# Idle TensorE products at the start of an attention-and-MLP kernel: nineteen in place of twenty-four, and sixteen of them ahead of the first mean product

## The chip, the core and the metric

The kernel runs on one core of one Trainium2 chip. The metric is the device time of one execution in microseconds (us), as the median of several runs; lower is better. Beside the timed runs there is one profiled execution, from which all the views below come. Its span is the time from its first to its last recorded instruction.

## The reference

The kernel computes one mixer block on x with 2048 tokens of 512 features, in float32. A sliding local attention with 32 heads of 16 features looks at 8 earlier positions in steps of 2; an MLP with 1376 hidden features gates it.

```python
xn = layernorm(x)
qkv = xn @ wqkv                                  # 512 -> 3 * 512
logits = q . k[pos - 2*w] * 16 ** -0.5           # w = 0..7, masked where pos - 2*w < 0
s = (softmax(logits) . v[pos - 2*w]) @ wo
h = gelu(layernorm(xn) @ w1 + b1)                # 512 -> 1376
g = silu(h @ w2 + b2)                            # 1376 -> 512
out = x + s * g
```

## The kernel before, in words

**Tiling.** The 2048 tokens are split by parity c (0 or 1) and then into 8 tiles of 128 tokens each. Attention runs in eight units (c, hb), where hb is a block of 8 heads; the MLP runs over four chunks of 512 tokens and eleven blocks of hidden features. Nearly every product on TensorE (PE) is done three times, in float16: each float32 operand is split into a high and a low half, and high·high, high·low and low·high are summed in PSUM. The lines that carry this work are L864 (qkv), L1143 (first MLP product), L1186 (second MLP product) and L1056 and L1088 (the product with wo).

**The start.** Before the float16 halves exist, two tiles of parity 0 (tiles 6 and 7) take another way. They are loaded already transposed (L1258, tensor `in_A_xt_dram`, into `U`), and each is centred: a product with a constant 128x128 matrix of 1/512 (`mean1`, in the tile `first`) gives the mean over the features, and VectorE (DVE) subtracts it in L693. For tile 6 DVE sums the four feature blocks first (L685) and PE multiplies once (L691, the first mean product); for tile 7 PE does four products (L682). The centred tile is multiplied in float32 with the raw weights of hb 0 (L700, four products a tile). The other tiles are loaded by L1233 into `prod` and go through statistics on DVE (L659, L660, L714, L716), a power on GpSimd (POOL, L718), a normalisation on one of three engines (L744 on ScalarE, written ACT here; L748 on POOL; L751 on DVE), a transpose on PE (L766), and the split into halves (L770 or L772 for the high half, L773 for the low half). Only then can L864 use them. The weights of hb 0 get a common scale on the way: ACT sums squares (L597), PE adds these up over the partitions (L513), DVE makes the scale (L524 to L542), ACT and DVE or POOL make the halves (L619; L626 or L553 and L554). Results of L864 leave PSUM by L882 (ACT) or L878 (DVE).

**The idle products.** Line 1305 makes products whose result nobody reads: the stationary operand is the constant tile `fours` (bfloat16, 128x128), the moving operand is `mean1` seen as 256 columns of bfloat16, and the result goes to the PSUM bank z0. They need nothing but the two constants that DVE sets at the start (L439, L440), and, where z0 was used by something else, that its reader is done. Their number is the constant `WAKE`:

```python
for n in range(WAKE):                                          # L1303
    b = R_z[0].new()
    pl.add("pe", 0.2, lambda b=b: nc.tensor.matmul(b.t[:, 0:2 * P], fours, mean1.bitcast(BF16), start=True,
                                                   stop=True), [], [b], prio=1e9)
```

**What sets the order.** All operations are first added to a plan (`Plan.add`), in which each has its number, engine, reads and writes. `Plan.issue` then walks through the tuple `ORDER`, which names every operation once by its number, picks a buffer of each ring for it and issues it on its engine:

```python
order, fixed = [], [self.ops[n] for n in reversed(ORDER)]      # L296
```

So each engine executes its share of `ORDER` in that sequence. An instruction that waits for a semaphore holds up everything behind it on its engine. The loads all go through the queue of SyncE (SP), in the sequence of the tuple `LOADS`, and SP uses eight semaphores in turn, so that the ninth load is issued when the first has landed, and so on.

Of the kernel before, what the change touches and what calls it, by code (L numbers as in the profile page):

```python
# [70 lines left out]
BEFORE_W1 = (0, 1, 4, 5)  # L71

ORDER = (
# [62 lines left out]
)  # L136


class Buf:


    def __init__(self, ring):
        self.ring, self.slot, self.left, self.end = ring, None, 0, 0.0
# [224 lines left out]
PU1 = 0.969  # L368
PWARM = 0.9
PEV = 0.2698  # L370

PTOT = 0.5899

WAKE = 24
PS1 = 1.1561

QHI = 4

PQLO = 0.5225

# [1146 lines left out]
```

## Time and profile before

| what | us |
|---|---|
| median of 3 timed runs | 413.33 (413.10 to 413.67) |
| the profiled execution's own time | 412.45 |
| its span, first to last instruction | 410.6 |
| PE busy in it | 403.6 |
| DVE busy | 381.7 |
| ACT busy | 225.3 |
| POOL busy | 132.8 |

A row of the timeline reads: start and duration in us from the span's start, engine, line, operation, what it writes `<-` what it reads, size, how many in a row, and in brackets the engine's idle time before it with what ended it. Where a row merges several instructions, the duration is that of the whole row. Matmuls are pipelined: each is recorded for longer than the distance to the next, so the rate is read from the distance between starts, not from the duration of one. LDWEIGHTS rows (PEld) are the loading of a stationary operand, beside the matmuls.

### The profile page before, as it was taken

The page shows a single profiled execution, that of the slowest core. Times are in us where ns is not written, and L with a number is a line of the kernel's source. Part 1 is how long each engine was busy: PE and PEld are TensorE (multiplying, and loading weights), DVE is VectorE, ACT ScalarE, POOL GpSimd, SP SyncE. Part 2 cuts the span into 40 slices and gives each one's busy share as a digit, 9 for nine tenths or more (in the row PEclk, how much of TensorE's full clock was granted, in tenths as well). Part 3 has the DMA queues.
Part 4 walks back from the last instruction along what each step waited for, and adds up shares of the span by engine and source line. Part 5 has one row for each costly group of instructions (what it writes and reads, how often), then busy time and mean ns, then how long its engine had stood idle before and what let it go on. Part 6 is the DMA issues. An engine that isn't in the chain of part 4 may idle for free.

```text
span 410.6 us, 5500 instructions
## 1 busy us (share of the span) xinstructions
PE 403.6 (98%) x2035; PEld 199.3 (49%) x2035; DVE 381.7 (93%) x386; ACT 225.3 (55%) x372; POOL 132.8 (32%) x141
## 2 busy tenths in 40 slices
PE   7999999999999999999999999999999999999996
PEld 4665544444444455445544554444445544444443
DVE  4999999999999999999889999899999989989985
ACT  4899987983989736633564164114523177236310
POOL 3833000053552434243423344233322505250012
PEclk9999999999999999999999999999999999999999
DMA  8947437240018372911251008610244462004874
GB/s 300 388 105 233 165 110 199 89 180 26 1 30 197 77 130 79 165 32 27 51 145 23 0 2 215 208 51 25 104 120 122 107 137 59 0 1 117 271 209 180
DMA packets 52627, 48.04 MB, mean 117 GB/s; under 512 B 37066, under 2 KB 37510, under 8 KB 52088
## 3 DMA queue, kind: packets, MB, share of 16 engines
q1 hardware_dynamic: 52600, 47.69, 41.8%
q8 instruction: 16, 0.26, 0.3%
q14 instruction: 11, 0.09, 0.1%
HBM read 24.40 MB, written 7.34 MB: 77 GB/s over the span
## 4 chain that ended last, share of the span: by engine, by line
PE 97%; DVE 1%; DMA 1%; ACT 0%; issue 0%; ACTq 0%; DVEq 0%
PE ps L864 30%; PE ps L1143 25%; PE z L1186 25%; PE ps L1056 5%; PE z L1088 2%; PE ps L1088 2%; PE z L1174 2%; PE pl L864 1%; PE pl L700 1%; DMA U<-in_A_xt_dram 1%; PE pl L1088 1%; PE z L700 1%; PE z L1177 1%; PE z L766 1%; PE z L1305 0%; DVE U L1120 0%
## 5 line engine op out<-in xcount | busy, mean ns | idle before, releaser
L864 PE MATMUL ps<-wq,yT 128*128 128x384 f16 (+1 forms) x708 | 129.3, 337 | 0.1
L1186 PE MATMUL z<-w,h 128*128 128x512 f16 x480 | 111.4, 379 | 0.0
L1143 PE MATMUL ps<-yT,w 128*128 128x512 f16 x480 | 109.1, 379 | 0.0
L864 PEld LDWEIGHTS <-yT 128*128 128x128 f16 x744 | 72.3, 98 | 58.5 <-issue 1.1
L930 DVE TENSOR_TENSOR prod<-U 128x2048 f32<-128x2048 f32 x32 | 73.8, 2312 | 4.1 <-ACT U L882 3.0
L1143 PEld LDWEIGHTS <-w 128*128 128x128 f16 x480 | 46.7, 98 | 55.6 <-issue 0.5
L933 DVE TENSOR_REDUCE L<-prod 128x128 f32<-128x2048 f32 x32 | 73.0, 2282 | 0.5
L1186 PEld LDWEIGHTS <-h 128*128 128x128 f16 x480 | 46.5, 98 | 54.6 <-issue 0.7
L999 POOL TENSOR_TENSOR prod<-prod,prod 128x1024 f32<-128x1024 f32 x14 | 41.3, 2970 | 81.4 <-DVE prod L988 81.4
L882 ACT ACTIVATE U<-ps,cs 128x384 f32<-128x384 f32 x54 | 30.2, 577 | 62.9 <-PE ps L864 62.7
L988 DVE TENSOR_TENSOR prod<-pl,U 128x2048 f32<-128x2048 f32 x28 | 63.5, 2283 | 0.3
L1156 ACT ACTIVATE ps<-ps,b1T,hsc 128x512 f32<-128x512 f32 x40 | 29.9, 748 | 37.2 <-PE ps L1143 37.0
L1159 ACT ACTIVATE h<-ps,hsc 128x512 f16<-128x512 f32 x40 | 27.4, 685 | 20.5 <-PE z L1186 19.5
L1009 POOL COPY gate<-prod 1x1 f32<-1x1 f32 x21 | 4.6, 221 | 102.2 <-DVE prod L930 102.2
L1010 POOL TENSOR_TENSOR prod<-prod 128x1024 f32<-128x1024 f32 x14 | 32.8, 2346 | 0.0
L1161 DVE SCALAR_TENSOR_TENSOR h<-ps,hsc,h 128x512 f16<-128x512 f32 x40 | 29.5, 744 | 3.3 <-ACT h L1159 3.3
L1056 PE MATMUL ps<-wo,oT 128*128 128x512 f16 x96 | 21.5, 379 | 0.0
L983 DVE TENSOR_TENSOR prod<-prod,prod 128x2048 f32<-128x2048 f32 x9 | 20.6, 2288 | 0.2
L971 ACT ACTIVATE o<-prod,osc 128x1024 f16<-128x1024 f32 (+1 forms) x9 | 9.5, 1052 | 18.1 <-DVE prod L983 9.9
L1010 POOL TENSOR_TENSOR prod<-prod,prod 128x1024 f32<-128x1024 f32 x7 | 16.4, 2347 | 0.0
L1088 PEld LDWEIGHTS <-oT 128*128 128x128 f16 x108 | 10.5, 98 | 10.4 <-issue 0.2
L1056 PEld LDWEIGHTS <-oT 128*128 128x128 f16 x96 | 9.4, 98 | 11.1
(201 smaller groups left out, 397.2 us busy)
## 6 DMA issues: line engine op xcount, KB each, us to landing
f<-in_A_x_dram SPq DMA_DIRECT2D x31, 256.0 KB, 3.1
U<-U SPq DMA_DIRECT2D x16, 392.0 KB, 6.2
gd<-f SPq DMA_DIRECT2D x12, 256.0 KB, 4.3
prod<-in_A_x_dram SPq DMA_DIRECT2D x8, 256.0 KB, 6.2
oT<-in_B_w_dram SPq DMA_DIRECT2D x2, 1024.0 KB
yT<-in_B_w_dram SPq DMA_DIRECT2D x2, 1024.0 KB
f<-gd SPq DMA_DIRECT2D x8, 256.0 KB, 5.0
out_dram<-f SPq DMA_DIRECT2D x8, 256.0 KB
```

Of the source, the lines that this page charges most:

```text
L864: nc.tensor.matmul(b.t[:, 0:wide], y[:, s, k, o:o + P], wq[hb][:, t, k], start=(n == 0), stop=(n == 11))
L882: act(384, lambda i=i, b=b: nc.scalar.activation(U3[:, i:i + 31:15, :], b.t[:, 0:384].rearrange("p (t e) -> p t e", t=3), AF.Identity, sca ...
L930: dve(2048, lambda p2=p2, g=g: nc.vector.tensor_tensor(p2(), q, slots(Ut, KH, 2 * g), op=ALU.mult), qk + [("kh", ub, 0), ("kh", ub, 1), (" ...
L933: dve(2048, lambda pr=pr, g=g: nc.vector.tensor_reduce(L3()[:, 2 * g:2 * g + 2], pr.t.rearrange("p (r f d) -> p r f d", r=2, d=DH), AX.X, ...
L988: dve(2048, lambda: nc.vector.tensor_tensor(pr.t.rearrange("p (r f d) -> p r f d", r=2, d=DH), A3()[:, 2 * g:2 * g + 2].rearrange("p r (f ...
L999: pool(2.4, lambda n=n: nc.gpsimd.tensor_tensor(acc.t[:, n:n + 1024], acc.t[:, n:n + 1024], p1.t[:, n:n + 1024], op=ALU.add), [acc, p1], [ ...
L1010: nc.gpsimd.tensor_tensor(x.t[:, 0:1024], x.t[:, 0:1024], y(), op=ALU.add)
L1056: nc.tensor.matmul(b.t, oT[:, hb, i // 4, s, i % 4], wo[:, t, hb], start=(hb == 0 and n == 0), stop=(hb == last and n == 2))
L1088: nc.tensor.matmul(b.t[:, cols], oT[:, hb, i // 4, s, i % 4], wo[:, t, hb, cols], start=(start and hb == 0 and n == 0), stop=(stop and hb ...
L1143: nc.tensor.matmul(b.t[0:M], w1[:, s, f * 512 + k * M:f * 512 + (k + 1) * M], yT[ch][:, t, k], start=(n == 0), stop=(n == 11))
L1156: act(512, lambda: nc.scalar.activation(b.t[0:M], b.t[0:M], AF.Gelu_apprx_tanh, bias=b1T[0:M, f:f + 1], scale=hsc[0:M, 1:2]), [b, ("b1T",) ...
L1186: nc.tensor.matmul(z.t, hl[s][:, t * P:(t + 1) * P], w2[:, w, f], start=(f == 0 and n == 0), stop=False)
```

## The change

`WAKE` goes from 24 to 19, and the idle products stand at other places of `ORDER`. Since five operations fewer are added to the plan, every operation behind them has a number that is lower by five, and so the whole tuple is written anew. The sequence of all other operations is the same: DVE, ACT, POOL and SP execute the same instructions in the same order, and PE the same apart from L1305.

```diff
 ORDER = (
-    0, 1, 240, 19, 2, 3, 4, 5, 6, 7, 8, 9, 10, 11, 133, 129, 113, 120, 112, 115, 130, 20, 21, 32, 33, 168, 114,
+    0, 1, 235, 19, 2, 3, 4, 5, 6, 7, 8, 9, 10, 11, 110, 111, 112, 113, 114, 115, 116, 117, 118, 119, 120, 121,
...
-WAKE = 24
+WAKE = 19
```

Before, PE's sequence had seven idle products ahead of L691 and three behind it, and fourteen further on: one between the products of L700 for tile 6, three and one around the L513 ahead of the first transpose, one, two and one around the first eight products of L864, one behind the next four, and one each near 21.7, 40.7, 48.1 and 56.0 us of the profiled execution. Now there are sixteen ahead of L691, the same three behind it, and none further on. So nine are added at the start, and fourteen are taken out later.

The first place, on PE, is the float32 product of tile 6 and the sum of squares behind it (`pl` is the PSUM bank of tile 6, `s` holds the sums of squares). The difference there reads:

```order
 L700 MATMUL pl_146<-prod_100,U_94 128x384 x2
-L1305 LDWEIGHTS fours
-L1305 MATMUL z_147<-first,fours 128x256
 L513 LDWEIGHTS fours
 L513 MATMUL z_147<-s_126,fours 128x1
```

L513, for whose result DVE waits, now stands directly behind the two products of L700.

The second place, on PE, is in the stage in which the first MLP product (`w`, `yT`) alternates with the qkv products of hb 1 (`wq_83`):

```order
 L1143 LDWEIGHTS w_86
 L1143 MATMUL ps_143<-yT_89,w_86 128x512
-L1305 LDWEIGHTS fours
-L1305 MATMUL z_147<-first,fours 128x256
 L864 LDWEIGHTS yT_90
 L864 MATMUL ps_144<-wq_83,yT_90 128x384
```

Here an idle product stood between two products of the real work, and now these follow each other. The places near 21.7, 40.7 and 56.0 us look the same with other neighbours.

122 rows, old and new, of the table ORDER are left out of this document.

## Prediction

> **What bounds the kernel now.** I read the page first: its busy times and the chain that ended last.
>
> ```profile
> PE 403.6 (98%) x2035; PEld 199.3 (49%) x2035; DVE 381.7 (93%) x386; ACT 225.3 (55%) x372; POOL 132.8 (32%) x141
> ...
> PE 97%; DVE 1%; DMA 1%; ACT 0%; issue 0%; ACTq 0%; DVEq 0%
> ```
>
> The chain of waits is PE almost from end to end, so PE time taken out comes off the span, unless PE then stands waiting for DVE or ACT. That splits the question by stage. The table by stage says where the others have room:
>
> ```profile
> 4.50:9.20 4.70, 4.52 (x13) 2.46 (x13) 2.59 (x6) 2.57 (x5) 0.40 (x1) 1.00 1.03 373
> 22.00:62.00 40.00, 39.97 (x227) 21.88 (x225) 38.11 (x59) 37.30 (x65) 6.24 (x10) 1.00 0.54 160
> 62.00:390.00 328.00, 327.91 (x1632) 157.77 (x1631) 313.27 (x261) 171.24 (x280) 108.57 (x107) 1.00 0.36 93
> ```
>
> The columns are PE, PEld, DVE, ACT and POOL busy (with instructions), granted clock, DMA share and GB/s. From 62 us on PE is without a gap and ACT is half idle: whatever PE has won by then it keeps. From 22 to 62 us DVE (38.1 of 40) and ACT (37.3 of 40) are nearly as full as PE, so an idle product taken out there counts only where they don't hold PE up. What happens before 22 us is in the timeline of PE:
>
> ```profile
> 1.19 1.65 PE L1305 MATMUL z<-first,fours 128*128 128x256 bf16 x7 [1.19 <-DVE first L440]
> 4.54 0.80 PE L691 MATMUL ps<-f,first 128*128 128x128 f32 x2 [1.70 <-DVE f L685]
> 5.13 0.85 PE L1305 MATMUL z<-first,fours 128*128 128x256 bf16 x3
> 6.11 2.93 PE L700 MATMUL pl<-prod,U 128*128 128x384 f32 x4
> 8.83 0.42 PE L1305 MATMUL z<-first,fours 128*128 128x256 bf16 x1
> ...
> 9.90 1.05 PE L682 MATMUL ps<-U,first 128*128 128x128 f32 x8
> ...
> 11.44 0.49 PE L1305 MATMUL z<-first,fours 128*128 128x256 bf16 x3
> ...
> 12.33 2.75 PE L700 MATMUL z<-prod,U 128*128 128x384 f32 x8
> 15.10 0.66 PE L766 MATMUL z<-first,prod 128*128 128x128 f32 x4
> ...
> 17.51 0.66 PE L766 MATMUL z<-first,prod 128*128 128x128 f32 x4
> ...
> 21.73 0.27 PE L1305 MATMUL z<-first,fours 128*128 128x256 bf16 x1
> ```
>
> Two things are to be seen. First, PE runs at half speed until about 9.2 us: three idle products at 5.13 have starts 0.215 us apart, (0.85 - 0.42)/2, with the 0.42 of the single one at 8.83; three at 11.44 are 0.11 apart, (0.49 - 0.27)/2, with the 0.27 of the one at 21.73. The single one at 8.83 is still recorded at the slow length, and L682's eight records at 9.90 are already 0.11 apart, (1.05 - 0.27)/7, so the change lies between. L700 likewise takes 2.93 for four records at 6.11 and 2.75 for eight at 12.33. The granted clock of 1.00 in the row of 4.5 to 9.2 us doesn't show this; the distances do. The doubling comes 4.6 us after PE's last long gap (1.70 us, ended at 4.54). Second, the seven idle products leave PE idle from 2.84 to 4.54, waiting for DVE's sum L685.
>
> **The nine products added at the start.** Sixteen at 0.215 from 1.19 end at 4.63, and L691 starts at 4.54 now. So L691 slips by 0 to 0.09 us; I take 0.05. It is hidden, as the next part shows. What they do is close the gap: PE is then busy without a long break from 1.19. If the doubling again comes 4.6 us after that start, it comes at 5.8 in place of 9.2; the bounds are "no earlier than before" (9.2) and "at the first real product" (4.6).
>
> **What the earlier doubling is worth.** Here is DVE, and below it SP:
>
> ```profile
> 9.36 0.16 DVE L524 TENSOR_SCALAR ssq<-z 128x1 f32<-128x1 f32 x1 [0.71 <-PE z L513]
> ...
> 9.87 0.69 DVE L659 BATCH_NORM_STATS2 bn<-prod 128x6 f32<-128x512 f32 x1
> 10.60 0.18 DVE L660 BATCH_NORM_AGGREGATE mv<-bn 128x2 f32<-128x6 f32 x1
> 10.99 0.69 DVE L693 TENSOR_TENSOR U<-U,ps 128x512 f32<-128x512 f32 x1 [0.21 <-PE ps L682]
> 11.59 0.69 DVE L659 BATCH_NORM_STATS2 bn<-prod 128x6 f32<-128x512 f32 x1
> ...
> 17.81 0.14 DVE L542 TENSOR_SCALAR qsc<-s 128x1 int32<-128x1 int32 x1
> 18.20 0.69 DVE L772 CAST yT<-z 128x512 f16<-128x512 f32 x1 [0.24 <-PE z L766]
> ```
> ```profile
> 9.18 0.33 SPq L1233 DMA_DIRECT2D prod<-in_A_x_dram x1
> 9.86 0.33 SPq L1260 DMA_DIRECT2D h<-in_B_w_dram x1
> ```
>
> With the clock up at 5.8, L700's four records (0.34 each) end near 7.6 and L513 near 7.8, so DVE's wait of 0.71 for L513 goes. What is late next is a load. SP issues at 9.18 and 9.86 what has waited for the loads of tile 7 and of one x tile to land; L659 needs the latter and starts at 9.87 whatever PE does. L682 needs tile 7: from 9.18 its eight records (1.05) end by 10.25. DVE is at L693 when L660 ends, 10.60 + 0.18 = 10.78, and starts it at 10.81 in place of 10.99. **The whole start is worth 0.18 us**, since loads hold DVE before and after. If the clock comes up only at 9.2, the idle product taken out at 8.83 still moves L682 by 0.21, and a slip of 0.09 leaves 0.12: L693 then starts near 10.87. So this term lies between 0.12 and 0.18 by the profiled run.
>
> Does DVE keep it? From 11.59 to 17.81 there are 22 rows of DVE, the first and the last shown, none with idle time before it. At 18.20 it waits for the transposes, which PE starts at 17.51 behind DVE's own L751. So PE's start at 17.51, and what follows from it, is set by DVE and moves by 0.18 and no more: the nine idle products taken out between 11.44 and 18.65 (about 1.0 us of PE at 0.11 each) are filled with waiting and bring **nothing**.
>
> **The last four places.** These two rows are of ACT, PE and the group of idle products between 40 and 62 us:
>
> ```profile
> 34.21 0.56 ACT L882 ACTIVATE U<-pl,cs 128x384 f32<-128x384 f32 x1
> ...
> 41.37 0.19 ACT L782 ACTIVATION_READ_ACCUMULATOR f<-f 128x1 f32 x1
> 41.63 0.58 ACT L882 ACTIVATE U<-ps,cs 128x384 f32<-128x384 f32 x1
> ```
> ```profile
> 34.83 2.11 PE L864 MATMUL pl<-wq,yT 128*128 128x384 f16 x12
> ```
> ```profile
> L1305 PE MATMUL z<-first,fours 128*128 128x256 bf16 x3 | 0.8, 272 | 0.0
> ```
>
> The product at 21.73 gives 0.11, but at 34.83 PE starts as L882 ends (34.21 + 0.56 = 34.77), on an ACT that is dense there; ACT has moved by DVE's 0.18 alone, so the 0.11 is lost. The one at 40.67 meets the next such place: ACT ends L782 at 41.56 and starts L882 at 41.63, when PE's results are there. PE would be 0.29 earlier, ACT 0.18; L882 gains up to 0.25, and I take 0.23, that is 0.05 on top. The bounds are 0 and 0.11. The last two (48.1 and 56.0) stand between dense products with no wait behind them: 0.11 each, 0.22 (bounds 0 and 0.22).
>
> **Sum:** 0.18 + 0.05 + 0.22 = 0.45 us less, bounds 0.12 and 0.51. The profiled execution took 412.45 (span 410.6), so it would take 412.0 (410.15). The median of the timed runs, 413.33, lies 0.88 above it; less 0.45 that gives **412.9**. A difference under 0.2%, 0.83 us, I count as none, about what a measurement of this kernel can tell from no change.
>
> **Rivals.**
>
> *More is gained.* The moment at which the clock doubled is known for one execution. If it was later in the timed ones, L682 and L693 were later by half of that, with all behind them; the 0.88 us between the median and the profiled time would be explained by a doubling 1.8 us later, near 10.9. With PE busy from 1.19 such a delay stays harmless, since the doubling then has until 9 us. The timed median would fall by up to 0.88 + 0.45, to 412.0. For it speaks that the profiled run is below all three timed ones; against it, that the difference can come from anything else, loads above all. [...]
>
> [...]
>
> *Slower: the clock drops again.* The products taken out kept PE busy in waits, one of them for POOL:
>
> ```profile
> 9.48 2.08 POOL L748 TENSOR_SCALAR prod<-prod,mv,rb 128x512 f32<-128x512 f32 x1
> ```
>
> Without them PE stands idle from about 8.3 (L700 done) to 9.2 (tile 7 landed), and again from 11.0 to 11.6, where the first transpose waits for L748 to end: 1.5 us of the 3.4 between 8.2 and 11.6. If that is enough to halve the clock, the eight records of L700, which start near 12.0 then, take twice 2.75 at worst; with half of them slow they end near 16.1 in place of 15.0, and L766, now at 15.10, starts near 16.3: 1.2 us late on the chain that DVE follows. That gives 413.33 + 1.2 = 414.5. It decides from the share of idle time at which the clock falls, which no row here shows: the 1.70 us gap fell in the slow time already. [...]
>
> *The change doesn't raise the clock sooner.* Worked out above: 0.12 in place of 0.18, so 412.95, inside the forecast.
>
> **How the numbers follow.** The forecast, with the rival that the clock comes no sooner, 412.75 to 413.05: 0.5. More, 412.0 to 412.6: 0.25. Nothing, 413.1 to 413.5: 0.15. Slower, 414.5: 0.10. The range 412.1 to 413.5 leaves out the slower case and the far end of the second. Faster by over 0.2% is below 412.5, which is most of the second case: 0.23; slower by over 0.2% is the last case: 0.10; the rest, 0.67, is within.
>
> **What would show it.** Right: L1305 x16 in a row from 1.19, L691 at 4.5 to 4.65, idle products or L700 at the fast rate before 8 us, no wait of DVE L524 for L513, L693 at 10.8, PE's transposes at 17.33 in place of 17.51, and from 62 us PE about 0.45 ahead row by row. Wrong: L693 of tile 7 at 11 or later, L700 for tile 7 at half speed, waits of PE between 42 and 62 us that weren't there, or a gain lost behind 62 us, where I take PE to wait for none.

## The result, and the profile after

The kernel after takes **412.25 us** (median of 20 runs, 411.60 to 413.17); the kernel before, timed beside it, 413.16 us (20 runs, 412.48 to 413.86). The ratio is 0.9982, with a 95% interval of 0.9976 to 0.9988, so 0.74 us less (0.5 to 1.0); the two medians differ by 0.91, which lies in that interval too. By the ratio this is just inside the 0.83 us that the prediction counted as no difference, by the medians just outside, and the time lies in its range. Gains of the timed runs are told by the ratio from here on. It does not lie in the forecast's own 412.75 to 413.05, but in that of the first rival, *more is gained* (412.0 to 412.6).

The profiled execution hides this: it took 412.82 us with a span of 411.0, more than the 410.6 of before. So it has to be read stage by stage. The page first, busy times and chain:

```profile
PE 402.8 (98%) x2030; PEld 198.7 (48%) x2030; DVE 381.6 (93%) x386; ACT 224.9 (55%) x372; POOL 132.7 (32%) x141
...
PE 90%; DVE 3%; ACT 3%; DMA 1%; POOL 1%; issue 0%; SPq 0%; POOLq 0%; ACTq 0%; DVEq 0%
```

PE has five products and 0.8 us less. The table by stage (PE, PEld, DVE, ACT and POOL busy, granted clock, DMA share, GB/s):

```profile
4.50:9.20 4.70, 3.92 (x15) 2.00 (x13) 2.18 (x5) 1.87 (x4) 0.00 (x0) 1.00 1.01 350
22.00:62.00 40.00, 39.87 (x225) 21.81 (x224) 38.24 (x61) 37.41 (x65) 6.77 (x11) 1.00 0.57 155
62.00:390.00 328.00, 327.91 (x1632) 157.79 (x1631) 313.39 (x261) 171.62 (x280) 108.53 (x107) 1.00 0.37 94
```

From 62 us PE is as dense as before (327.91 of 328). PE is idle for 0.78 us between 4.5 and 9.2, where it was idle for 0.18: two waits of 0.27 and 0.29 us, for DVE and for ACT, and the start of a longer one. PE's timeline of the start:

```profile
1.19 3.57 PE L1305 MATMUL z<-first,fours 128*128 128x256 bf16 x16 [1.19 <-DVE first L440]
4.64 0.79 PE L691 MATMUL ps<-f,first 128*128 128x128 f32 x2
5.23 0.72 PE L1305 MATMUL z<-first,fours 128*128 128x256 bf16 x3
6.21 1.56 PE L700 MATMUL pl<-prod,U 128*128 128x384 f32 x4 [0.27 <-DVE U L693]
...
10.12 1.16 PE L682 MATMUL ps<-U,first 128*128 128x128 f32 x8 [1.14 <-DMA U<-in_A_xt_dram]
...
12.61 0.66 PE L766 MATMUL z<-first,prod 128*128 128x128 f32 x4 [0.69 <-POOL prod L748]
13.11 2.75 PE L700 MATMUL z<-prod,U 128*128 128x384 f32 x8
```

Sixteen idle products in a row lead into L691 without a gap. The four records of L700 at 6.21 take 1.56 us, where they took 2.93: the clock is already up, and the trace's record of the granted clock has its first entry at 5.68 us, where before has 9.20. Then PE waits, 1.14 us for tile 7 and 0.69 us for POOL (both between 8.98 and 12.61), and the eight records of L700 at 13.11 still take 2.75 us: the clock did not drop. DVE and SP in the same stretch:

```profile
9.57 0.15 DVE L524 TENSOR_SCALAR ssq<-z 128x1 f32<-128x1 f32 x1
...
10.77 0.69 DVE L659 BATCH_NORM_STATS2 bn<-prod 128x6 f32<-128x512 f32 x1 [0.61 <-DMA prod<-in_A_x_dram]
...
11.60 0.67 DVE L693 TENSOR_TENSOR U<-U,ps 128x512 f32<-128x512 f32 x1
...
18.93 0.69 DVE L772 CAST yT<-z 128x512 f16<-128x512 f32 x1 [0.25 <-PE z L766]
```
```profile
10.09 0.33 SPq L1233 DMA_DIRECT2D prod<-in_A_x_dram  x1
10.77 0.33 SPq L1260 DMA_DIRECT2D h<-in_B_w_dram  x1
```

DVE's waits for PE at L524 (0.71) and at L693 (0.21) are gone, as predicted. But this L659 waits for its load, which landed 0.9 us later in this execution than in that of before (SP issues at 10.77 what it issued at 9.86). What follows is later for that reason, less what the change gained: L693 by 0.61 us (10.99 before) and L772 by 0.73 (18.20 before). A load's landing is nothing that the change touches, and other executions below show that it varies so by itself.

### The profile page after: what moved, and what is told of

It is laid out like the page before. It is cut to its first block, busy times and chain, and to the rows that moved or that the text cites. A ratio compares the mean times of both kernels' runs of the same rounds, so it can differ in the third digit from the quotient of the medians.

```text
span 411.0 us, 5490 instructions
## 1 busy us (share of the span) xinstructions
PE 402.8 (98%) x2030; PEld 198.7 (48%) x2030; DVE 381.6 (93%) x386; ACT 224.9 (55%) x372; POOL 132.7 (32%) x141
## 4 chain that ended last, share of the span: by engine, by line
PE 90%; DVE 3%; ACT 3%; DMA 1%; POOL 1%; issue 0%; SPq 0%; POOLq 0%; ACTq 0%; DVEq 0%
PE ps L864 27%; PE z L1186 25%; PE ps L1143 25%; PE ps L1056 5%; PE z L1088 2%; PE ps L1088 2%; PE z L1174 2%; DMA prod<-in_A_x_dram 1%; DVE bn L659 1%; ACT w L565 1%; ACT w L504 1%; PE pl L1088 1%; PE z L1177 1%; PE pl L864 1%; POOL prod L748 1%; DVE yT L773 0%
## 5 line engine op out<-in xcount | busy, mean ns | idle before, releaser
L864 PE MATMUL ps<-wq,yT 128*128 128x384 f16 (+1 forms) x708 | 128.9, 337 | 0.2
L864 PEld LDWEIGHTS <-yT 128*128 128x128 f16 x744 | 72.2, 98 | 59.1 <-issue 1.3
L882 ACT ACTIVATE U<-ps,cs 128x384 f32<-128x384 f32 x54 | 30.1, 575 | 62.9 <-PE ps L864 62.7
```

The lines of the kernel that those rows point to most:

```text
L864: nc.tensor.matmul(b.t[:, 0:wide], y[:, s, k, o:o + P], wq[hb][:, t, k], start=(n == 0), stop=(n == 11))
L882: act(384, lambda i=i, b=b: nc.scalar.activation(U3[:, i:i + 31:15, :], b.t[:, 0:384].rearrange("p (t e) -> p t e", t=3), AF.Identity, sca ...
```

## How the executions are compared

Since the landings differ, each trace is read between fixed rows of DVE. Behind the start that is from L772 to DVE's last row, the last of L1127; here in before and in after:

```profile
407.47 0.42 DVE L1127 TENSOR_TENSOR U<-U 128x256 f32<-128x256 f32 x1
```
```profile
407.87 0.42 DVE L1127 TENSOR_TENSOR U<-U 128x256 f32<-128x256 f32 x1
```

For before that is 407.47 - 18.20 = 389.27 and for after 407.87 - 18.93 = 388.94: **0.33 us gained behind the start**. (The expectations count to the span's end, where these two read 392.44 and 392.11.)

In the start two loads lead to L772. One is that of the third L659 (9.87 in before, 10.77 in after; the expectations call it the eighth load, by its place in SP's queue), with tile 7 beside it and L693 behind it. The other is that of the first L659, with x tile 0 behind it, then POOL's power and L748, a transpose, ACT's L770 and DVE's L773. In after the rows of the second chain are these, of DVE:

```profile
7.76 0.69 DVE L659 BATCH_NORM_STATS2 bn<-prod 128x6 f32<-128x512 f32 x1 [1.60 <-DMA prod<-in_A_x_dram]
...
13.28 0.61 DVE L626 SCALAR_TENSOR_TENSOR wq<-prod,qsc,wq 128x384 f16<-128x384 f32 x1
13.92 0.69 DVE L773 TENSOR_TENSOR yT<-z,yT 128x512 f16<-128x512 f32 x1
```

L773 stands 0.64 us behind L626; in the run without idle products, where the clock holds DVE longest, it is 0.52 (13.86 and 14.38). So L773 waits here for 0.12 us, too short for a bracket, and what it waits for comes from POOL. From the first L659 to L772 is 18.93 - 7.76 = 11.17 in after, and the same 11.17 in five other executions. Where the third L659 decides, as in out_40 and swap4, it is 8.03 from there to L772. The later of the two sums gives the start that the loads allow; what L772 is later than that is lost to the clock. All runs, with ratios to the kernel before, timed beside each:

| run | clock up at | first L659 | third L659 | loads allow L772 at | L772 | lost | L772 to last row | median | ratio (95% interval) |
|---|---|---|---|---|---|---|---|---|---|
| before | 9.20 | 6.35 | 9.87 | 17.90 | 18.20 | 0.30 | 389.27 | 413.16 | 1 |
| after | 5.68 | 7.76 | 10.77 | 18.93 | 18.93 | 0 | 388.94 | 412.25 | 0.9982 (0.9976 to 0.9988) |
| before_again | 7.90 | 8.13 | 11.14 | 19.30 | 19.30 | 0 | 389.27 | 413.14 | 1.0002 (0.9992 to 1.0011) |
| late_out | 9.53 | 6.93 | 9.91 | 18.10 | 18.38 | 0.28 | 388.94 | 412.59 | 0.9991 (0.9982 to 1.0000) |
| nine_only | 6.70 | 6.95 | 9.94 | 18.12 | 18.12 | 0 | 389.26 | 412.53 | 0.9990 (0.9981 to 0.9999) |
| mid_out | 8.56 | 7.07 | 10.07 | 18.24 | 18.24 | 0 | 389.26 | 412.84 | 0.9995 (0.9987 to 1.0004) |
| none | 11.79 | 7.01 | 10.00 | 18.18 | 19.39 | 1.21 | 388.94 | 413.29 | 0.9999 (0.9990 to 1.0008) |
| 24_ahead | 5.42 | 7.00 | 10.05 | 18.17 | 18.17 | 0 | 389.15 | 412.45 | 0.9992 (0.9983 to 1.0001) |
| after_again | 6.04 | 6.80 | 9.82 | 17.97 | 17.97 | 0 | 388.94 | 412.10 | 0.9979 (0.9970 to 0.9987) |
| swap1 | 5.71 | 7.16 | 9.47 | 18.33 | 18.34 | 0.01 | 388.94 | 412.25 | 0.9977 (0.9968 to 0.9986) |
| swap4 | 4.91 | 6.68 | 9.73 | 17.76 | 17.76 | 0 | 390.37 | 412.07 | 0.9973 (0.9962 to 0.9984) |
| swap3 | 6.84 | 7.53 | 9.84 | 17.87 | 18.09 | 0.22 | 388.93 | 411.88 | 0.9965 (0.9953 to 0.9978) |
| out_21 | 8.23 | 6.77 | 9.97 | 18.00 | 18.01 | 0.01 | 389.26 | (one time, 412.22) | |
| out_40 | 7.95 | 6.70 | 9.90 | 17.93 | 17.93 | 0 | 389.16 | (one time, 412.04) | |

In swap3 and swap4 the first L659 reads x tile 0 itself, so the sum with 11.17 doesn't apply to them, and only the third L659 is counted; the 0.22 us of swap3 belong to another chain, told below, and not to the clock. The clock's moment is the first entry of the trace's record of the granted clock.

## The experiments

The theory at this point was that of the prediction: the nine products at the start raise the clock sooner, which is worth a little until loads bind; the middle ones bring nothing; of the last four some count. The expectations call it *the sum*. The rivals were that more hangs on the clock than one execution shows (*the late clock*), and that the idle products do nothing at the start. In the diffs below the rows are the sequence of an engine.

**The kernel before, once more** (no edit; its file has one line more, so that L1305 is L1306 there).

> The kernel before, unchanged, as a measure of what two equal kernels differ by, and as a second look at its start. Both theories: 0, within 0.3 us. They differ in the profile. 'The sum' (the start is worth 0.18 us, the later products 0.27) expects the TensorE clock to double near 9.2 us after the first instruction again, and VectorE's L693 of tile 7 to be held up by L682 for 0.2 us. [...]

Ratio 1.0002 (0.9992 to 1.0011). The clock came up at 7.90, and L772 stands where the loads allow it (8.13 + 11.17 = 19.30). So the start of before loses 0.30 us in one execution and nothing in another.

**The last four taken out of the kernel before** (one of the places below).

```diff
-WAKE = 24
+WAKE = 20
...
 L864 MATMUL ps_144
-L1305 MATMUL z_147<-first,fours 128x256
 L864 MATMUL ps_144
```

> Only the four last idle products (near 21.7, 40.7, 48.1 and 56.0 us) are taken out; the start is that of before. Both 'the sum' and 'the late clock': 0.27 us faster (0.2 to 0.44). If the whole gain of the change came from these four, 0.75 to 0.9 us faster. In the profile the time from L693 of tile 7 to the end should shrink by 0.27 us.

From L772 on 388.94, the number of the kernel after to the hundredth: the 0.33 us behind the start come from these four alone. Its start, that of before, met the latest clock of its kind (9.53), and L772 is 0.28 us behind the loads.

**The nine added ahead, and nothing taken out.**

```diff
-WAKE = 24
+WAKE = 33
...
+L1305 MATMUL z_147<-first,fours 128x256 x9
 L1305 MATMUL z_147<-first,fours 128x256 x7
 L691 MATMUL ps_143<-f_103,first 128x128
```

> Only the nine idle products ahead of the first mean product are added; all 24 of before stay. 'The sum': the clock doubles near 5.7 us, L693 of tile 7 no longer waits for TensorE, 0.18 us faster. 'The late clock': 0.45 to 0.6 us faster, since the timed runs lost more to the clock than the profiled one. If the nine do nothing: 0.

Ratio 0.9990 (0.9981 to 0.9999), 0.41 us less (0.04 to 0.79). With late_out's 0.37 (0 to 0.74) the sum is 0.78, close to the 0.74 of the whole change. With such intervals this fits parts that add up, and does not show it; nor does it tell the 0.18 us of *the sum* from the 0.45 to 0.6 of *the late clock*.

**The middle ten taken out** (all between 8.8 and 18.7 us; the first place below).

```diff
-WAKE = 24
+WAKE = 14
...
 L700 MATMUL pl_146<-prod_100,U_94 128x384 x2
-L1305 MATMUL z_147<-first,fours 128x256
 L513 MATMUL z_147<-s_126,fours 128x1
```

> Only the ten idle products between 8.8 and 18.7 us are taken out: seven and three at the start stay, and the last four. 'The sum': these fill waits, so 0 to 0.15 us faster (the one at 8.83 held up L682 by 0.21), and the clock doubles when it does in the kernel before. 'The late clock': the same or a little slower, 0 to 0.1. If these ten cost TensorE time of their own, as many as 1.0 us faster. If they kept the clock up, slower by 1 us or more, with products at half rate after 9.2 us in the profile.

Behind L772 389.26, unchanged, and L772 where the loads allow it, with the clock up at 8.56. The ratio, 0.9995 (0.9987 to 1.0004), allows anything from a gain of 0.5 to a loss of 0.2 us. The clock did not drop: the mean granted clock of this execution is 1.000, where 1.61 us behind the end of the fast stretch make it 0.998 in late_out.

**No idle product at all.**

```diff
-WAKE = 19
+WAKE = 0
```

> No idle product is made at all (WAKE is 0); everything else stands in the same order. Against the kernel before, taking out the four late ones gains 0.33 us, as the runs without them showed behind L772. What the start then costs tells the theories apart. Theory A (the nine products ahead of L691 are worth little, because loads hold DVE whatever PE does): the clock doubles near 9 to 10 us, the start loses 0.1 to 0.3 us, and the median falls 0.0 to 0.2 us below that of the kernel before, 0.5 to 0.8 above the kernel after. Theory B (without idle products the clock stays halved past the load of tile 7, so that L682 and L700 of tile 7 run at half speed): the doubling comes at 10 to 13 us, L772 lies 9 us or more behind the landing of the eighth load in place of 8.2, and the median is 0.2 to 1.5 us above the kernel before. Theory C (the idle products at the start do nothing): L772 lies 8.2 us behind the landing, and the median equals that of the kernel after, 412.3 to 412.6.

Here are PE and then DVE of that run:

```profile
4.59 0.79 PE L691 MATMUL ps<-f,first 128*128 128x128 f32 x2 [4.59 <-DVE f L685]
6.17 2.93 PE L700 MATMUL pl<-prod,U 128*128 128x384 f32 x4 [0.78 <-DVE U L693]
...
10.41 1.72 PE L682 MATMUL ps<-U,first 128*128 128x128 f32 x8
```
```profile
10.00 0.69 DVE L659 BATCH_NORM_STATS2 bn<-prod 128x6 f32<-128x512 f32 x1 [0.21 <-DMA prod<-in_A_x_dram]
...
12.17 0.69 DVE L693 TENSOR_TENSOR U<-U,ps 128x512 f32<-128x512 f32 x1 [1.25 <-PE ps L682]
```

L700 and L682 run at the slow rate, the clock comes up only at 11.79, and DVE waits 1.25 us at L693: L772 is 1.21 us behind the loads. This shows what the idle products at the start do, and it is Theory B's trace. The median (413.29) lies a little lower than B had it: by the timed runs, to 0.4 us either way, what the start lost against before took back the 0.33 us of the last four.

**Twenty-four ahead of L691 in place of sixteen.**

```diff
-WAKE = 19
+WAKE = 27
...
+L1305 MATMUL z_147<-first,fours 128x256 x8
 L1305 MATMUL z_147<-first,fours 128x256 x16
 L691 MATMUL ps_143<-f_103,first 128x128
```

> As the kernel after, but with 24 idle products ahead of L691 in place of 16: at 0.215 us each they end near 6.3 us, so that L691 slips from 4.6 to about 5.5 to 6.3 (the clock doubles on the way, which makes the last ones cheaper). Theory A (the loads bind the start, as the prediction had it, and L691 is hidden): L693 of tile 7 and L772 stay where the eighth load puts them, 8.2 us between landing and L772, and the median is that of the kernel after within 0.3 us, with a ratio of 0.998 to 0.999 against the kernel before. Theory B (L691 is on the path by way of L693 of tile 6 and what DVE has behind it): 1.0 to 1.7 us later than the kernel after at L772, and 0.3 to 1.0 us above the kernel before.

PE and then DVE of that run:

```profile
1.19 4.83 PE L1305 MATMUL z<-first,fours 128*128 128x256 bf16 x24 [1.19 <-DVE first L440]
5.86 0.39 PE L691 MATMUL ps<-f,first 128*128 128x128 f32 x2
```
```profile
6.28 0.69 DVE L693 TENSOR_TENSOR U<-U,ps 128x512 f32<-128x512 f32 x1 [1.72 <-PE ps L691]
...
10.05 0.69 DVE L659 BATCH_NORM_STATS2 bn<-prod 128x6 f32<-128x512 f32 x1 [0.66 <-DMA prod<-in_A_x_dram]
...
43.48 2.29 DVE L930 TENSOR_TENSOR prod<-U 128x2048 f32<-128x2048 f32 x1 [0.72 <-DMA U<-U]
```

L691 slips by 1.2 us and L693 of tile 6 by 0.8, yet the third L659 still waits 0.66 us for its load, and L772 is where the loads allow it (7.00 + 11.17): in this execution loads hide a slip of a whole microsecond (just so: L693 ends as the first L659 can start, 7.00), and the 0.1 us of the change is hidden with much room. With a first x tile that lands sooner, as in before (6.35), the large slip would show, and in the timed runs it seems to: the ratio is 0.9992 (0.9983 to 1.0001), where after_again, timed beside the same executions of before, has 0.9979. That is 0.5 us more, and the median lies 0.35 us above after_again's and 0.20 above that of after, where Theory A allowed 0.3. In the profiled execution 0.21 us are missing behind L772 (389.15 for 388.94); they were lost at 43.48, where DVE waited for a copy within the chip; no other trace here has that wait.

**The kernel after, once more** (no edit).

> The kernel after without any edit, for a second profile and a second comparison beside the other runs of this call. Expected: 0.5 to 1.0 us below the kernel before (ratio 0.9976 to 0.9988); the clock doubles between 4.6 and 8 us; DVE does not wait for PE at L693 of tile 7; L772 lies 8.2 us behind the landing of the eighth load, and 392.1 us ahead of the end. If the term at the start is only the 0.18 us of one execution, the ratio is 0.9988 (0.33 + 0.18 us); if the clock doubles later on average in the kernel before, it is 0.998 or below.

```profile
6.80 0.69 DVE L659 BATCH_NORM_STATS2 bn<-prod 128x6 f32<-128x512 f32 x1 [0.75 <-DMA prod<-in_A_x_dram]
...
9.82 0.69 DVE L659 BATCH_NORM_STATS2 bn<-prod 128x6 f32<-128x512 f32 x1 [0.62 <-DMA prod<-in_A_x_dram]
10.55 0.18 DVE L660 BATCH_NORM_AGGREGATE mv<-bn 128x2 f32<-128x6 f32 x1
10.65 0.68 DVE L693 TENSOR_TENSOR U<-U,ps 128x512 f32<-128x512 f32 x1
...
17.97 0.69 DVE L772 CAST yT<-z 128x512 f16<-128x512 f32 x1 [0.24 <-PE z L766]
```

These are DVE's rows. The third L659 starts within 0.05 us of its start in before, and L693 stands 0.83 us behind it, where it stood 1.12 behind it in before (10.99 - 9.87): **0.29 us gained at L693**. At L772 0.18 us of that are left (8.15 for 8.33), because the first L659 came 0.45 us later than in before and now decides (6.80 + 11.17). The median, 412.10, and the ratio, 0.9979 (0.9970 to 0.9987), repeat the result.

**One load moved.** The next three aim at the loads that bind. The first moves the first weight load of hb 1 (384 KB by the profile, not the 256 of the expectation) behind that of tile 7. SP's rows, and ACT's:

```diff
-L588 DMA U_94<-in_A_wqkv_dram 128x768
 L1258 DMA U_94<-in_A_xt_dram 128x512
 L1233 DMA prod_102<-in_A_x_dram 128x512
+L588 DMA U_94<-in_A_wqkv_dram 128x768
...
-L597 ACTIVATE wq_83,s_127<-U_94 128x768
 L619 ACTIVATE wq_82<-prod_100,qsc 128x384 x4
+L597 ACTIVATE wq_83,s_128<-U_94 128x768
```

> The kernel after with one load moved: the first weight load of hb 1 (256 KB) is issued behind those of tile 7 and of the next x tile in place of ahead of them, and what reads it (ACT's L597 for hb 1 and PE's first L513 of hb 1) moves behind it. Theory A (the start is bound by the landing of the eighth load, and a load ahead of it costs it time): the loads of tile 7 and x land 0.3 to 0.7 us earlier, L772 with them, and the median is 0.3 to 0.6 us below that of the kernel after. Theory B (the queue lands its loads at a fixed pace of issue and the place of one changes nothing, or ACT is late with L597 and what follows): the same median as the kernel after, or up to 1 us above it.

PE and then DVE:

```profile
8.52 1.16 PE L682 MATMUL ps<-U,first 128*128 128x128 f32 x8
9.51 0.81 PE L700 MATMUL pl<-prod,U 128*128 128x384 f32 x2
12.01 0.66 PE L766 MATMUL z<-first,prod 128*128 128x128 f32 x4 [1.69 <-POOL prod L748]
```
```profile
9.47 0.68 DVE L659 BATCH_NORM_STATS2 bn<-prod 128x6 f32<-128x512 f32 x1
...
13.32 0.69 DVE L773 TENSOR_TENSOR yT<-z,yT 128x512 f16<-128x512 f32 x1 [0.75 <-ACT yT L770]
```

L682 starts 0.64 us sooner than in after_again and the third L659 0.35 (8.52 and 9.47, from 9.16 and 9.82). The loads landed about 0.6 us sooner, as Theory A had it (SP's issues that wait for them are at 8.49 and 9.20, from 9.13 and 9.81), but L772 did not follow. PE waits 1.69 us for POOL's L748, and DVE 0.75 us for what follows it. L772 is at 7.16 + 11.17: the chain by way of x tile 0 and POOL decides. The median is that of the kernel after.

**POOL's chain sooner, alone and together with the moved load.** swap4 loads x tile 0 ahead of x tile 2 and takes its statistics first (DVE's rows):

```diff
 L660 BN_AGGR mv_153<-bn_139 128x2
+L714 TENSOR_SCALAR pb_154<-mv_153 128x1
 L659 BN_STATS bn_140<-prod_101 128x6
 L660 BN_AGGR mv_153<-bn_140 128x2
-L714 TENSOR_SCALAR pb_154<-mv_153 128x1
```

> The kernel after with x tile 0 loaded ahead of x tile 2 and its statistics and L714 ahead of those of tile 2, and nothing else moved. Theory A (in the kernel after the chain of tile 7 by way of L693 binds, and POOL's L748 has just as much room as it needs): L748 and the first transpose come about 0.7 to 0.9 us sooner, PE's wait for L748 goes, and L772 and the median stay (within 0.1 us at L772 for the same landings). Theory B (POOL's L748 binds): L772 comes 0.3 us sooner or more, and so does the median.

POOL, PE and ACT:

```profile
8.61 2.07 POOL L748 TENSOR_SCALAR prod<-prod,mv,rb 128x512 f32<-128x512 f32 x1
```
```profile
10.74 0.65 PE L766 MATMUL z<-first,prod 128*128 128x128 f32 x4
...
14.75 0.66 PE L766 MATMUL z<-first,prod 128*128 128x128 f32 x4 [0.62 <-ACT prod L744]
```
```profile
50.16 1.91 ACT L504 ACTIVATE w<-yT 128x2048 bf16<-128x2048 f32 x1 [2.34 <-DMA yT<-in_B_w_dram]
```

L748 comes 0.9 us sooner than in after_again (9.53), and PE's wait for it is gone. L772 is 8.03 us behind the third L659, where it was 8.15 in after_again: 0.12 us gained, and the other load decides. So POOL's chain binds in the two traces of the kernel after, with 0.12 us to the next, and the median (412.07) cannot tell that from nothing. The profiled execution lost 1.43 us elsewhere (390.37 for 388.94): ACT waited 2.34 us at 50 us for a load of 1 MB that the other executions hardly wait for.

swap3 has both edits of swap1 and swap4, with ACT's L597 of hb 1 behind the first L770.

```diff
 L770 CAST yT_89<-z_150 128x4x128
-L597 ACTIVATE wq_83,s_127<-U_94 128x768
+L597 ACTIVATE wq_83,s_128<-U_94 128x768 x2
 L742 ACTIVATE rb_155<-pb_154,rb_155 128x1
```

> The kernel after with the load order of swap1 and the chain that held swap1 started sooner: x tile 0 is loaded ahead of x tile 2, its statistics and L714 stand ahead of those of tile 2 on DVE, and ACT's L597 of hb 1 stands behind the first L770. Theory A (the start has two chains of nearly the same length, one from the load of tile 7 by way of L693, one from x tile 0 by way of POOL's L718 and L748; swap1 shortened the first alone): L718 starts about 1 us sooner than in swap1 (8.2 in place of 9.2), DVE's wait of 0.75 us at the first L773 is gone, L772 starts 0.3 to 0.5 us sooner than in the kernel after with the same landings, and the median is 0.3 to 0.5 us below it. Theory B (a third chain, ACT's or the x tiles 1, 3 and 4, ends just behind): L772 and the median stay where they are in the kernel after, within 0.2 us.

PE and then DVE:

```profile
15.61 0.66 PE L766 MATMUL z<-first,prod 128*128 128x128 f32 x4 [0.78 <-ACT prod L744]
```
```profile
12.90 0.69 DVE L773 TENSOR_TENSOR yT<-z,yT 128x512 f16<-128x512 f32 x1
```

DVE's wait at L773 is gone, and a third chain shows, ACT's L744: PE waits 0.78 us for it, and L772 is 0.22 us behind what the third L659 allows. In this execution the first x tile landed late (first L659 at 7.53), so the trace does not decide between the theories. The median, 411.88 us (5 runs), is the lowest of all, with a ratio of 0.9965 (0.9953 to 0.9978) to the kernel before; its interval overlaps that of the kernel after (0.9976 to 0.9988), so that it beats before is shown, and that it beats after only likely.

**Single products.** The last two kernels are the kernel before without the product at 21.73, and without that at 40.67.

```diff
-WAKE = 24
+WAKE = 23
```

> The kernel before without the one idle product at 21.73 us. By the prediction its 0.11 us is lost at the wait of L864 for ACT's L882: from L772 to the end 392.44 us as in the kernel before, with that wait 0.25 us in place of 0.15. If the 0.11 us is kept, 392.33. [...]

> The kernel before without the one idle product at 40.67 us. The prediction gave this product 0.05 us (0 to 0.11); the trace of the kernel after says that it counts in full: from L772 to the end 392.33 us in place of 392.44, with the wait near 42.9 us unchanged at 0.18. If it is lost, 392.44. [...]

PE in the run without the product at 21.73, and then in the kernel after:

```profile
34.34 0.17 PE L518 MATMUL ps<-s,fours 128*128 128x1 bf16 x1
34.62 2.11 PE L864 MATMUL pl<-wq,yT 128*128 128x384 f16 x12
```
```profile
35.27 0.17 PE L518 MATMUL ps<-s,fours 128*128 128x1 bf16 x1
35.55 2.11 PE L864 MATMUL pl<-wq,yT 128*128 128x384 f16 x12
```

In both, L864 stands 0.28 us behind L518; in before it is 0.19 (34.83 behind L518 at 34.64). PE came 0.1 us sooner, and waited 0.1 us longer for ACT's L882. From L772 on it is 389.26, nothing gained. Without the product at 40.67 it is 389.16, which is 0.11 less: that one counts in full.

## Why the prediction was right, and where it fell short

**The steps of the start** hold one by one: sixteen in a row from 1.19, L691 at 4.64 and 4.55, the clock at 5.68 and 6.04 (forecast 5.8), no wait at L524 or L693, transposes behind DVE. That the clock came so near 5.8 is luck: the rule behind it, 4.6 us after PE's start, does not hold. With the same start from 1.19 us the clock came up anywhere from 4.91 (swap4) to 6.84 (swap3), and with the start of before 3.35 us after L691 (before_again, 4.55 to 7.90) to 4.96 (late_out, 4.57 to 9.53). The forecast needed only that it came before 9. The slip of L691, 0.1 us, is hidden.

**The middle products, 0.** Right in the traces: 389.26 behind L772 in mid_out, and L772 where the loads allow it, no sooner.

**The last four.** The product at 21.73 is lost at ACT's L882, as forecast; those at 48.1 and 56.0 give 0.22, as forecast. The one at 40.67 was put at **0.05** and is worth 0.11: the wait at 41.63 holds ACT, not PE, and PE runs on.

**Where it was off.** Of the 0.65 us between the 412.9 of the forecast and 412.25, 0.17 come from its base: the three runs that it started from had a median of 413.33, the twenty beside the kernel after 413.16. The rest is the step *the whole start is worth 0.18 us*, once as shown and once as is likely. First, its size in the execution it was worked out for. L693 was put at 10.81, behind the recorded end of L660 (10.60 + 0.18); but L693 starts 0.10 us behind L660's start (10.55 and 10.65 above), since a recorded duration reaches into the next instruction. With the loads of before the start would have ended at 17.90, which is **0.30** sooner, so the whole sum for that execution is 0.30 + 0.33 = 0.63 where the forecast had 0.45 and 0.51 at most. The chain by POOL was not in the forecast at all; in after it takes 0.12 us of this back when its load comes late.

Second, and likely only, the step from one execution to the median. The loss of before is 0 in the executions with the clock up at 7.90, 7.95 and 8.56, 0.01 at 8.23, 0.30 at 9.20 and 0.28 at 9.53; in the kernel without idle products it is 1.21 at 11.79. In the timed runs the start is worth 0.74 - 0.33 = 0.41 (0.2 to 0.7), in after_again 0.87 - 0.33 = 0.54 (0.2 to 0.9), and in nine_only 0.41 (0.04 to 0.79). All three lie above 0.30, but each interval holds it, and 0.18 lies inside that of nine_only and at the lower end of the other two. The time that came is that of the rival *more is gained* and not of the likeliest case. The rival's mechanism, a clock that comes at another moment in each execution and costs the start when it is late, is in the traces; how much of the timed gain it makes is argued in what follows.

Does the clock's moment explain 0.41? By the trace's record of the granted clock it stayed up, from its first entry to its end, for 399.36 us (late_out), 402.77 (before) or 406.19 (after) in the executions here. What sets the moment at which it comes up is not shown.

Nor is it shown how that moment is spread over the timed executions. In the six profiled ones with the start of before (in mid_out, with the first ten of its products) it lies between 7.90 and 9.53 us, and they lose 0.10 us on average. The other executions left no trace, but for those timed with the experiments the span and the mean granted clock are on record. In the traces that mean is lower by half of the share of the span that lies behind the end of the fast stretch: 1.61 of 410.5 us in late_out, and the mean is 0.998. Of the 90 such executions of the kernel before, 20 have 0.998, so their fast stretch ended 1.2 to 2.1 us ahead of the span's end. Counted back by 399.36 us, their clock came up between 9.4 and 11.5 us (an estimate; by the next longer stretch, 402.77, it would be 6.0 to 8.1, and 7.90 is the earliest that a trace with this start shows). They took 413.26 us on average and the 56 with a mean of 1.000 took 413.02, which is 0.24 us less (0.07 to 0.41). In the four runs with at least sixteen products ahead of L691 and the last four out (after, after_again, swap1, 24_ahead) the same split gives 412.37 (15 executions) and 412.29 (31), next to nothing. By this count a late clock occurs in about a fifth of the timed executions of the kernel before, and costs time there. That it makes the whole of the 0.41 us is not shown.

**The rivals that fell.** *Slower: the clock drops again*: in after PE stood idle for 1.14 and 0.69 us within 3.63 (8.98 to 12.61), and L700 at 13.11 is fast; in swap1 the eight records of L700 take the same 2.75 us behind even 1.69 us in one piece. At what gap the clock would fall is not shown. *Nothing* (413.1 to 413.5): 388.94 us behind L772 in after, after_again, late_out and none, so the 0.33 us are kept to the end.

## What to carry to other kernels

A term read from one execution holds for that execution's luck: where a step depends on a moment that the kernel does not set, as the clock's or a load's, read it at several moments and weigh them before the sum is held against a median. Compare traces between fixed events (from the load to the first real work, from there to the end) rather than by their spans, which here differed by 0.4 us in the wrong direction. And a product that nobody waits for is free only while its engine waits: the same 0.11 us was nothing at 21.73, where ACT was next, and all of 0.11 at 40.67.

## What the hardware showed that was not expected

The landing of the same load varies by 1.3 us between executions of nearly the same kernel (that L659 starts between 9.82 and 11.14 where its load was in the same place), more than the change is worth. A load of 1 MB that ACT needs at about 48 us has next to no room: ACT waited 0.38 us for it in before_again, 0.15 in none, 0.19 in swap3 and 2.34 in swap4, so a start that is made sooner still can be lost there. In the execution without idle products PE worked from 4.59 on with one bracketed gap, of 0.78 us, and the clock came up only at 11.79, 7.2 us later; in those with the start of before it came 3.35 to 4.96 us behind the start of L691.
